# Two score buffers shared with the transposes, one PSUM bank for state products and y, and a new order of steps

## The chip, the cores and the metric

The kernel runs on one core of a Trainium2 chip. A core has five engines that work side by side, each through its own list of instructions in order: TensorE (PE in the profile; its weight loads are PEld), VectorE (DVE), ScalarE (ACT), GpSimd (POOL) and SyncE (SP), which here only issues DMAs. Matmul results go to PSUM, which has eight banks of 2 KB per partition; the other operands lie in SBUF. The metric is the time of the kernel on the device in microseconds, lower is better.

## The reference

An attention without softmax, with a decaying state, runs along the sequence, and a layer norm with a two-layer network follows. There are 4 batches, 8 heads, 768 positions and 48 values per head; the model width is 8 x 48 = 384.

```python
for t in range(S):
    kt, vt, rt = (k[:, :, t].copy(), v[:, :, t].copy(), r[:, :, t].copy())
    cur = np.einsum('bhd,bhe->bhde', u[None] * kt, vt)
    y[:, :, t] = np.einsum('bhd,bhde->bhe', rt, state + cur)
    state = w[None, :, :, None] * state + np.einsum('bhd,bhe->bhde', kt, vt)
...
xn = (x - mu) / np.sqrt(var + 1e-06) * g_ln
ch = np.maximum(xn @ w_ch1, 0.0) @ w_ch2
return (x + ch).astype(np.float32)
```

## The kernel before

The sequence of each batch is cut into 6 chunks of 128 positions: 24 chunks, numbered 0 to 23. Two neighbouring chunks make a pair, 12 pairs. Within a chunk the recurrence is computed as masked products of r and k (scores) times v; between chunks the state is handed on. The first two pairs (chunks 0 to 3) are worked on together with steps of their own, whose names end in 2. Then the chunk's rows pass through the network, in 18 groups of one or two chunks.

The steps that the text names, by chunk i, pair g or group:

- LK, LR, LV, LK2, LR2, LV2 load k, r and v; LW1 loads a third of the first weight matrix, SW scales one slice of it to bf16 (three slices to a third, so LW1,2 feeds SW,6 to SW,8), IW2 loads the second matrix by a DMA from GpSimd's queue. WF, UF and LG load w, u and the norm's gain. CV2 casts v.
- SK, SR, SK2, SR2 multiply k and r by powers of w. TRk and TRr transpose the results on TensorE into PSUM, TCk and TCr copy them to SBUF; from pair 5 on, TDk and TDr transpose by DMA instead. Q2 multiplies the two transposes.
- AT and AT2 compute the scores of one chunk (8 or 16 matmuls into two banks), AM and AM2 mask them into SBUF (VectorE). S computes the state product of a chunk, and for a pair's first chunk also the diagonal terms; CC2 copies those out, VB2 multiplies v by them, ZU and ZD make the next state.
- Y and Y2 compute y of a chunk, X adds VB2's part and sums the row, SQ the squares, XN centres the row, RS makes the norm's factor. LT transposes the row on TensorE and XT copies it out; from group 8 on, LTD does it by DMA.
- UP is one bank of the first matrix product (index 16 x group + part), RL its relu into SBUF, DN a third of the second product of a chunk (index 4 x chunk + part), OT scales and adds, STO stores. DU are filler matmuls on zeros that nothing waits for; WBM and COL spread w over the partitions at the start.

The order is written out by hand in the string PLAN (lines 18 to 66): `name,index,engine`, where the engine is v (VectorE), s (ScalarE), g (GpSimd) or - (TensorE, or a DMA on SyncE's queue). Lines 751 to 753 emit the steps in this order, so each engine gets its list in the order of PLAN, and semaphores make a step wait for its inputs and for the last readers of the buffer that it writes.

PSUM before: `hp` has two buffers of one bank (UP), `at` one buffer of two banks (AT, AT2), and one bank each go to `tr` (TRk, TRr, LT), `s` (COL, S), `y` (WBM, Y, Y2) and `o` (DU, DN). That makes eight.

Of the kernel before, what the change touches and what calls it, by code (L numbers as in the profile page):

```python
# [28 lines left out]
XT,3,v SW,4,s AT,6,- CC2,2,s SK,9,g RL,32,v UP,48,- SQ,0,s LV,8,- AM,6,v UP,50,- RL,48,s SW,3,g TRk,4,- SQ,2,s RL,50,v  # L29
UP,34,- IW2,1,g TCk,4,s LK,11,- SR2,4,v AT,7,- UP,1,- IW2,2,g RL,34,s VB2,2,v TRr,4,- RL,1,s DN,0,- ZU,4,v Q2,3,g LR2,5,-  # L30
TCr,4,s UP,33,- X,4,v AM,7,v XN,4,s Y,5,- UP,49,- RL,33,s CV2,3,v LT,4,- UP,17,- RL,49,s X,5,v XT,4,s S,6,- XN,5,g
RS,2,s Y,6,- AT,8,- ZU,6,v SQ,4,s UP,66,- RS,0,g AM,8,v CC2,3,s RL,17,s DN,1,- SQ,3,s LK,10,- S,7,- VB2,3,v LT,5,-
AT,9,- SQ,5,s DN,2,- X,6,v UP,64,- LR2,6,- OT,0,v XN,6,g Y,7,- RL,64,s Q2,4,v DN,4,- RL,66,s X,7,v RS,3,g LK,13,-
DN,5,- SQ,1,s XT,5,v DN,6,- SQ,6,s SR2,5,v UP,65,- LV,9,- RS,1,s LT,6,- XN,7,s OT,1,v UP,80,- SK,10,g RL,65,s ZU,7,v
DN,8,- LR2,7,- XT,6,s AM,9,v SK,11,g UP,82,- RS,4,g DN,9,- LK,12,- RL,80,v DN,10,- ZD,7,g LV,11,- UP,81,- CV2,4,s OT,2,v
SR2,6,g TRr,5,- TDk,5,- RL,82,v RS,5,s S,8,- TCr,5,s DN,12,- ZU,8,v DN,13,- RL,81,v SK,13,g LV,10,- CC2,4,s LT,7,- DN,14,-
SK,12,g XT,7,v TRr,6,- LV,12,- OT,3,v UP,114,- VB2,4,g TCr,6,v UP,112,- STO,0,- S,9,- RL,114,v Y,8,- ZD,8,g AT,10,- X,8,v
DN,16,- TDk,6,- Q2,5,g ZU,9,v XN,8,s DN,17,- AM,10,v CV2,5,s LV,13,- Y,9,- DN,18,- STO,2,- SQ,8,s X,9,v LK,15,- UP,96,-
ZD,9,g STO,1,- OT,4,v AT,11,- RL,96,s S,10,- Q2,6,v DN,20,- RL,112,s AM,11,v XN,9,g CC2,5,s DN,21,- VB2,5,g LTD,8,- UP,98,-
ZU,10,v DN,22,- RL,98,s SR2,7,v Y,10,- CV2,6,s UP,113,- STO,3,- ZD,10,g SQ,7,s UP,97,- OT,5,v LK,14,- LR2,8,- RL,113,v AT,12,-  # L40
RS,6,g RL,97,s DN,24,- LK,17,- X,10,v SQ,9,s RS,7,g S,12,- Y,11,- LV,14,- DN,25,- X,11,v UP,128,- XN,10,v XN,11,s LK,16,-
AM,12,v SK,14,g UP,129,- RL,128,s DN,26,- LTD,9,- SK,15,g RL,129,s UP,130,- OT,6,v UP,131,- SR2,8,v RL,130,s TRr,7,- RS,8,s CC2,6,v
RL,131,v DN,28,- VB2,6,g TDk,7,- ZU,12,v DN,29,- TCr,7,v DN,30,- AT,13,- SK,16,g OT,7,v UP,133,- LV,15,- UP,132,- LK,21,- RL,133,v
SK,17,g STO,4,- DN,32,- AM,13,v RL,132,s LV,16,- Y,12,- S,13,- STO,5,- DN,33,- X,12,v TDk,8,- AT,14,- Q2,7,v TRr,8,- UP,147,-
ZU,13,v TCr,8,s ZD,13,v DN,34,- RL,147,v XN,12,s Y,13,- UP,145,- OT,8,v CV2,7,s LR,19,- X,13,v UP,149,- RL,145,s XN,13,g S,14,-
SQ,12,s RL,149,v DN,36,- LTD,10,- SQ,11,s CC2,7,v AM,14,v UP,146,- VB2,7,g DN,37,- RL,146,s ZU,14,v AT,15,- SQ,10,s Y,14,- ZD,14,g
LV,17,- AM,15,v DN,38,- STO,6,- UP,144,- Q2,8,g LR,18,- X,14,v LK,20,- S,15,- AT,16,- OT,9,v RL,144,s LK,18,- Y,15,- RS,9,s
UP,148,- X,15,v SQ,13,s UP,164,- SK,21,g AM,16,v RL,148,s LR,20,- DN,40,- CV2,8,g ZU,15,v UP,161,- LK,19,- RL,164,v SR,19,g AT,17,-
RL,161,s S,16,- UP,160,- XN,14,s XN,15,v ZD,15,v DN,41,- RL,160,s LTD,11,- AM,17,v DN,42,- CC2,8,s UP,165,- ZU,16,v SK,18,g Y,16,-
OT,10,v UP,163,- STO,7,- RL,165,v SK,20,g LV,18,- DN,44,- RL,163,s STO,8,- VB2,8,v DN,45,- LV,19,- UP,162,- ZD,16,g X,16,v DN,46,-  # L50
RL,162,s SR,18,v UP,177,- RS,10,s OT,11,v XN,16,g TDr,9,- Y,17,- RL,177,s SK,19,g UP,180,- X,17,v SQ,15,s DN,48,- RL,180,v TDk,9,-
SQ,14,s DN,49,- CV2,9,g XN,17,s UP,178,- LR,21,- RS,11,g DN,50,- RL,178,s LTD,12,- UP,176,- SQ,16,s OT,12,v UP,179,- SR,20,v STO,9,-
RL,176,v DN,52,- TDk,10,- RL,179,s Q2,9,v DN,53,- SR,21,v DN,54,- AT,18,- S,18,- AM,18,v TDr,10,- UP,181,- UP,193,- RL,181,s ZU,18,v
AT,19,- OT,13,v RL,193,s Y,18,- UP,192,- STO,10,- AM,19,v CC2,9,s SQ,17,s LV,21,- DN,56,- LV,20,- S,19,- RL,192,v UP,194,- STO,11,-
VB2,9,v LV,23,- DN,57,- RL,194,s LK,23,- DN,58,- Q2,10,g X,18,v UP,195,- XN,18,s OT,14,v AT,20,- Y,19,- DN,60,- X,19,v CV2,10,g
DN,61,- AM,20,v XN,19,s DN,62,- SQ,18,s LTD,13,- ZU,19,v UP,197,- SQ,19,s OT,15,v ZD,19,g AT,21,- RL,195,s S,20,- DN,64,- LR,23,-
CC2,10,s RL,197,s ZU,20,v VB2,10,g STO,12,- UP,196,- AM,21,v LK,22,- S,21,- Y,20,- STO,13,- RL,196,s DN,65,- LR,22,- ZD,20,g RS,12,s
X,20,v LV,22,- DN,66,- SK,23,g UP,209,- OT,16,v Y,21,- XN,20,g ZU,21,v RL,209,s UP,213,- SR,23,v LTD,14,- UP,208,- SK,22,g RL,213,s
DN,68,- RS,13,s RL,208,v TDk,11,- UP,211,- X,21,v DN,69,- SR,22,v XN,21,s TDr,11,- RL,211,s DN,70,- SQ,21,s UP,210,- OT,17,v STO,14,-
UP,212,- RL,210,v LTD,15,- DN,72,- RL,212,v DN,73,- CV2,11,v UP,224,- STO,15,- UP,225,- RL,224,v STO,16,- DN,74,- ZD,21,v STO,17,- UP,226,-  # L60
OT,18,v AT,22,- Q2,11,v RL,226,s DN,76,- AM,22,v RL,225,s DN,77,- SQ,20,s S,22,- DN,78,- RS,14,g ZU,22,v AT,23,- CC2,11,s OT,19,v
Y,22,- VB2,11,g UP,240,- AM,23,v STO,19,- DN,80,- ZD,22,g X,22,v DN,81,- SQ,22,s DN,82,- XN,22,v RL,240,s LTD,16,- Y,23,- OT,20,v
UP,241,- RS,16,s X,23,v DN,84,- RL,241,s XN,23,v UP,242,- LTD,17,- RS,15,s SQ,23,s DN,85,- RL,242,v RS,17,s STO,18,- UP,258,- UP,256,-
RL,258,v DN,86,- RL,256,s UP,257,- OT,21,v UP,273,- STO,21,- RL,257,s STO,20,- DN,88,- RL,273,s DN,89,- UP,272,- DN,90,- RL,272,s UP,274,-
# [719 lines left out]
```

## Time and profile before

| | |
|---|---|
| median of three runs | 152.55 us (152.27 to 152.99) |
| the profiled execution | 152.22 us, of which the span from first to last instruction is 150.4 us |
| TensorE busy | 143.7 us, 96% of the span, 1960 matmuls |
| VectorE, ScalarE, GpSimd busy | 113.2, 83.1, 76.4 us |
| DMA | 26.92 MB, mean 179 GB/s, 16 DMA engines full in the first quarter of the span |
| TensorE clock granted | full speed throughout |

In the rows of the profile, a line such as `L545 PE MATMUL at<-trr,trk` names the source line, the engine, the operation and the tile written from the tiles read; then come the shapes, the count, the busy time in us with the mean of one in ns, and the idle time of the engine before them with what ended it. A timeline row begins with the start and the duration in us, counted from the first instruction; it merges neighbours of one kind, and the idle time before it stands in brackets. Matmuls overlap, so what a step costs TensorE is the distance from its start to the start of the next step.

### The profile page before, as it was taken

To read this page: it belongs to the slowest core of one execution; us is meant where nothing else is said; L and a number is where in the kernel's file an instruction comes from. 1 tells how busy PE (TensorE), PEld (TensorE's weight loads), DVE (VectorE), ACT (ScalarE), POOL (GpSimd) and SP (SyncE) were. 2 spreads that over 40 slices of the span, in tenths; PEclk is the share of its full clock that TensorE was granted. 3 is DMA by queue.
4 is the path that set the end of the run, shared out by engine and by line. 5 is a ranking of instruction groups with operands and counts; after the bars stand their busy time and mean duration, and the time that the engine had idled before them with its cause. 6 is when DMAs were issued, how large, how long until landed. Compare 5 with 4: busy or idle time off the path is not lost.

```text
span 150.4 us, 4721 instructions
## 1 busy us (share of the span) xinstructions
PE 143.7 (96%) x1960; PEld 112.5 (75%) x1963; DVE 113.2 (75%) x203; ACT 83.1 (55%) x185; POOL 76.4 (51%) x94
## 2 busy tenths in 40 slices
...
GB/s 106 309 314 324 290 242 261 215 196 257 233 211 160 65 166 167 160 195 179 124 213 175 138 148 196 198 188 187 187 188 67 241 160 185 140 52 52 118 91 56
DMA packets 84041, 26.92 MB, mean 179 GB/s; under 512 B 79282, under 2 KB 82484, under 8 KB 84020
## 3 DMA queue, kind: packets, MB, share of 16 engines
...
q10 hardware_dynamic: 402, 0.00, 0.2%
...
HBM read 18.88 MB, written 4.72 MB: 157 GB/s over the span
## 4 chain that ended last, share of the span: by engine, by line
PE 94%; DVE 4%; issue 1%
PE hp L647 31%; PE o L675 30%; PE o L271 6%; PE at L545 4%; PE tr L392 4%; PE s L482 3%; PE y L584 3%; PE y L505 2%; PE y L576 2%; PE s L461 2%; DVE xn L607 2%; PE at L435 1%; PE tr L632 1%; DVE A L554 1%; PE o L273 1%; PE o L690 1%
## 5 line engine op out<-in xcount | busy, mean ns | idle before, releaser
L647 PE MATMUL hp<-xT,w_sb 128*128 128x128 bf16 (+1 forms) x648 | 57.1, 237 | 0.0
L647 PEld LDWEIGHTS <-w_sb 128*128 128x128 bf16 x648 | 49.4, 114 | 4.0
L675 PE MATMUL o<-w_sb,hT 128*128 128x384 bf16 x276 | 52.4, 326 | 0.0
L663 ACT ACTIVATE hT<-hp 128x512 bf16<-128x512 f32 x49 | 28.9, 596 | 36.7 <-PE hp L647 36.4
L675 PEld LDWEIGHTS <-hT 128*128 128x128 bf16 x276 | 25.3, 98 | 12.5
L554 DVE TENSOR_TENSOR A<-at,mask 128x1024 bf16<-128x1024 f32 x20 | 24.4, 1218 | 1.3 <-PE at L545 1.3
L731 DVE SCALAR_TENSOR_TENSOR ot<-o,rs,x 128x384 f32<-128x384 f32 x23 | 14.2, 616 | 11.7 <-PE o L675 10.5
L202 POOL TENSOR_TENSOR sk<-kf,Fk 128x384 bf16<-128x384 f32 x18 | 19.1, 1075 | 5.7 <-ACT g_neg L296 4.8
L665 DVE TENSOR_SCALAR hT<-hp 128x512 bf16<-128x512 f32 x23 | 15.8, 688 | 4.8 <-PE hp L647 4.6
L591 DVE SCALAR_TENSOR_TENSOR x<-y,Vb 128x384 f32<-128x384 f32 x24 | 13.3, 553 | 5.2 <-PE y L584 3.0
L598 ACT ACTIVATE sqj<-x,sm 128x384 bf16<-128x384 f32 x24 | 14.7, 612 | 2.4 <-DVE x L591 2.2
L493 POOL TENSOR_TENSOR Vb<-vf,cc 128x768 f32<-128x768 f32 x8 | 11.8, 1480 | 8.0 <-ACT cc L197 4.1
L202 POOL TENSOR_TENSOR q<-trk,trr 128x1024 bf16<-128x1024 bf16 x5 | 10.7, 2138 | 6.7 <-DMA trr<-sr 6.7
L607 POOL TENSOR_SCALAR xn<-x,sm 128x384 bf16<-128x384 f32 x8 | 4.9, 614 | 17.9 <-DVE x L591 15.1
L271 PE MATMUL o<-warm 128*128 128x512 bf16 x31 | 10.2, 458 | 1.5 <-DVE warm L221 1.5
L605 ACT ACTIVATE xn<-x,sm 128x384 bf16<-128x384 f32 x11 | 6.8, 615 | 8.4 <-DVE x L591 8.4
L202 POOL TENSOR_TENSOR Z<-ZS,WLZ 128x384 bf16<-128x384 f32 x9 | 9.8, 1084 | 2.8 <-DVE ZS L566 2.8
L197 ACT COPY trr<-tr 128x512 bf16<-128x512 bf16 (+1 forms) x11 | 7.7, 766 | 5.9 <-PE tr L392 5.9
L202 DVE TENSOR_TENSOR sr<-rf,Fr 128x384 bf16<-128x384 f32 (+1 forms) x12 | 9.1, 764 | 2.2 <-ACT Fr L290 2.2
L202 POOL TENSOR_TENSOR sr<-rf,Fr 128x768 bf16<-128x768 f32 (+1 forms) x4 | 6.7, 1682 | 2.9 <-DMA rf<-in_r_dram 2.9
L566 DVE TENSOR_TENSOR ZS<-s,Z 128x384 f32<-128x384 f32 x12 | 6.6, 552 | 1.8 <-ACT cc L197 1.0
L545 PE MATMUL at<-trr,trk 48*128 48x128 bf16 x160 | 7.9, 219 | 0.0
...
## 6 DMA issues: line engine op xcount, KB each, us to landing
...
```

Source lines behind the costliest of these rows:

```text
L202: engines[e].tensor_tensor(out=out, in0=in0, in1=in1, op=ALU.mult)
L271: nc.tensor.matmul(out=warm_ps[0][:], lhsT=warm[:, :P], rhs=warm[:], start=True, stop=True)
L493: engines[e].tensor_tensor(out=Vb2(g).rearrange("p (x h d) -> p x h d", x=2, h=H), in0=vals, in1=cc2(g)[:].unsqueeze(3).to_broadcast([P, 2 ...
L545: nc.tensor.matmul(out=t[:, par, q, :], lhsT=trk(g)[p0 : p0 + D, a, q, :], rhs=trr(g)[p0 : p0 + D, a, q, :], start=True, stop=True,)
L554: nc.vector.tensor_tensor(out=AA(i)[:].rearrange("p e q t -> p (e q) t"), in0=psum["at", i][:].rearrange("p e q t -> p (e q) t"), in1=mask ...
L591: nc.vector.scalar_tensor_tensor(out=xx(i)[:], in0=psum["y", i][:, :C], scalar=1.0, in1=Vb(i), op0=ALU.mult, op1=ALU.add, accum_out=sm[i][:],)
L598: nc.scalar.activation(out=sqj[:], in_=xx(i)[:], func=ACT.Square, bias=sm[i][:], scale=-float(C), accum_out=sq[g][:, j : j + 1])
L647: nc.tensor.matmul(out=t[:, a * gw : (a + 1) * gw], lhsT=w1_sb[n][kc][:, fb::FB], rhs=xT(g)[:, :size, kc, :], start=(kc == 0), stop=(kc == ...
L663: nc.scalar.activation(out=o, in_=s, func=ACT.Relu)
L665: nc.vector.tensor_relu(out=o, in_=s)
L675: nc.tensor.matmul(out=psum["o", i][:, :C], lhsT=hT(g)[:, fk, j * P : (j + 1) * P], rhs=w2_sb[d][:, a, :], start=(fk == 0), stop=(fk == FK ...
L731: nc.vector.scalar_tensor_tensor(out=ot(i)[:], in0=psum["o", i][:, :C], scalar=rs[g][:, j : j + 1], in1=xx(i)[:], op0=ALU.mult, op1=ALU.add,)
```

## The change

PSUM is divided anew. `at` gets two buffers of two banks in a pool of its own, `ps_a`, and the transposes (TRk, TRr, LT) take their tiles from the same two buffers, of which they use half. S and Y share the one bank `y`. Y2, WBM and COL take their tiles from the two `hp` banks of the up-projection. `o` stays as it is. The sum is again eight banks.

PLAN has the same 749 steps in a new order. 113 of them change their engine or queue, among them: ten SK from GpSimd to VectorE and two the other way; three SW from ScalarE to VectorE and two to GpSimd (SW,0, SW,6 and SW,8 are on VectorE now, SW,1 to SW,3 on GpSimd); four ZD to VectorE and one from it; XN in 15 cases on GpSimd now, 6 on ScalarE and 3 on VectorE (before: 8, 11 and 5); three TCr from VectorE to ScalarE; 13 RL from VectorE to ScalarE and 11 the other way. The fillers DU keep their number and sizes. 16 of the 20 AT stand in pairs, one right behind the other on TensorE.

```diff
 PLAN = """
...
-LK2,0,- MP,4,g MM2,0,g LV2,0,- LN,0,s UWR,0,v DU,2176,- MP,3,v MO,0,v CV2,1,v LK2,1,- WBM,0,- COL,0,- LR2,1,- FR2,1,s FR2,0,s
-DU,2640,- SRH,1,v FK2,1,s SRH,0,v LK,5,- FK2,0,s UW,0,v SKH,1,v TRr,0,- UGC,0,s MP,0,v SKH,0,g DU,3120,- FR,0,s LR2,2,- TCr,0,v
-FK,0,s WL,0,s TRk,0,- LW1,0,- SK2,1,v DU,3616,- LV,5,- TCk,0,s SR2,1,v CV2,0,s LR2,3,- TRk,1,- AT2,0,- SK,4,v TCk,1,s Q2,0,v
-SK,5,v LW1,2,- S,0,- AM2,0,v SR2,2,g DU,576,- CC2,0,s TRr,1,- ZU,0,v TCr,1,s AT2,1,- LK,6,- DU,784,- AM2,1,v VB2,0,g S,1,-
-DU,576,- SW,0,s LK,7,- TRr,2,- ZU,1,v Y2,0,- TCr,2,s Q2,1,v AT2,2,- X,0,v DU,704,- SW,2,s LV,4,- TRk,2,- AM2,2,v XN,0,g
-Y2,1,- TCk,2,s SR2,3,g DU,576,- X,1,v AT2,3,- SW,1,s LT,0,- DU,464,- AM2,3,v S,2,- XT,0,s LW1,1,- XN,1,s UP,0,- LK,8,-
-ZU,2,v SW,7,s LT,1,- AT,4,- CC2,1,s SK,6,v LK,9,- XT,1,s Y2,2,- AM,4,v VB2,1,g SW,6,s S,3,- SW,8,s TRr,3,- ZU,3,v
-AT,5,- SK,7,g X,2,v TCr,3,s UP,16,- RL,0,v LR2,4,- Y2,3,- XN,2,g RL,16,s Q2,2,g TRk,3,- CV2,2,s X,3,v UP,18,- TCk,3,s
-AM,5,v UP,2,- LV,6,- RL,18,s LT,2,- XN,3,v IW2,0,g Y,4,- SW,5,s XT,2,v S,4,- RL,2,s LT,3,- SK,8,g LV,7,- UP,32,-
...
+SKH,0,v FR2,1,s SKH,1,g MP,5,v MP,0,v FR2,0,s DU,3120,- LV2,1,- UW,0,v WL,0,s SRH,1,v SRH,0,v TRk,0,- LR2,3,- SR2,1,v TRr,0,-
+TCk,0,s DU,3616,- LW1,0,- SR2,2,v LK,5,- TCr,0,s SK2,1,v TRr,1,- LV,5,- AT2,0,- TCr,1,s Q2,0,v DU,576,- AM2,0,v FK,0,s S,0,-
+FR,0,s AT2,1,- LK,7,- CC2,0,v ZU,0,v DU,784,- UGC,0,s VB2,0,g CV2,1,s TRk,1,- AM2,1,v S,1,- TCk,1,s DU,576,- SR2,3,v TRr,2,-
+LV,4,- Y2,0,- SK,4,v TCr,2,s SW,2,g ZU,1,v AT2,3,- LK,6,- Q2,1,v Y2,1,- SW,1,g X,0,v LW1,1,- TRr,3,- AM2,3,v LV,6,-
+SK,5,g S,2,- TCr,3,s LW1,2,- DU,704,- XN,0,g ZU,2,v LV,7,- X,1,v LT,0,- DU,576,- SW,0,v XT,0,s DU,464,- TRk,2,- CC2,1,s
+SQ,0,s AT2,2,- SK,6,g UP,0,- TCk,2,s AM2,2,v VB2,1,g S,3,- XN,1,s LR2,4,- RL,0,v AT,4,- CV2,2,s Y2,2,- ZU,3,v SK,7,g
+RS,0,s AM,4,v Y2,3,- SW,5,s SW,3,g SW,4,s Q2,2,v TRk,3,- LK,9,- X,2,v LT,1,- S,4,- TCk,3,s XT,1,v XN,2,g UP,1,-
+X,3,v CC2,2,v ZU,4,v UP,16,- XN,3,g RL,1,s IW2,0,g AT,5,- LK,8,- Y,4,- SW,8,v SW,7,s VB2,2,g SW,6,v LT,2,- RL,16,s
+AM,5,v UP,18,- LR2,5,- XT,2,s UP,2,- RL,18,s X,4,v LT,3,- Q2,3,v UP,34,- RL,2,s LV,9,- XN,4,g XT,3,v Y,5,- RL,34,s
+AT,6,- SR2,4,g X,5,v AT,7,- CV2,3,s UP,48,- AM,6,v UP,33,- RL,48,s LV,8,- SK,9,v S,6,- IW2,1,g RL,33,s UP,17,- ZU,6,v
...
+RL,208,s Y,20,- RL,211,s DN,64,- X,20,v SQ,19,s UP,212,- XN,20,g S,21,- SK,23,g DN,65,- ZU,21,v UP,209,- SK,22,v CV2,11,g RL,212,v
+Y,21,- TDk,11,- RL,209,s DN,66,- UP,210,- OT,16,v STO,13,- UP,213,- X,21,v RL,210,s DN,68,- XN,21,s RL,213,s DN,69,- LTD,15,- Q2,11,v
+RS,13,s DN,70,- ZD,21,v STO,14,- S,22,- OT,17,v AT,23,- LTD,14,- AT,22,- ZU,22,v DN,72,- AM,22,v DN,73,- STO,15,- DN,74,- CC2,11,v
...
@@ -101,6 +101,7 @@
     ps_h = ctx.enter_context(tc.tile_pool(name="ps_h", bufs=2, space=bass.MemoryType.PSUM))
+    ps_a = ctx.enter_context(tc.tile_pool(name="ps_a", bufs=2, space=bass.MemoryType.PSUM))
     ps = ctx.enter_context(tc.tile_pool(name="ps", bufs=1, space=bass.MemoryType.PSUM))
...
     def WBM(i, e):
-        t = psum["wb"] = ps.tile([P, 512], FP32, name="y")
+        t = psum["wb"] = ps_h.tile([P, 512], FP32, name="hp")
...
     def COL(i, e):
-        t = psum["col"] = ps.tile([P, 2, HP], FP32, name="s")
+        t = psum["col"] = ps_h.tile([P, 512], FP32, name="hp")[:, : 2 * HP].rearrange("p (a q) -> p a q", a=2)
...
     def turn(key, t):
-        psum[key] = ps.tile([P, 2 * HP, P], BF16, name="tr")
+        psum[key] = ps_a.tile([P, 4 * HP, P], BF16, name="at")[:, : 2 * HP, :]
...
     def AT2(i, e):
-        t = psum["at", i] = ps.tile([P, 2, HP, P], FP32, name="at")
+        t = psum["at", i] = ps_a.tile([P, 2, HP, P], FP32, name="at")
...
     def S_(i, e):
-        t = psum["s", i] = ps.tile([P, 512], FP32, name="s")
+        t = psum["s", i] = ps.tile([P, 512], FP32, name="y")
...
     def Y2(i, e):
-        t = psum["y", i] = ps.tile([P, 512], FP32, name="y")
+        t = psum["y", i] = ps_h.tile([P, 512], FP32, name="hp")
...
     def AT(i, e):
-        t = psum["at", i] = ps.tile([P, 2, HP, P], FP32, name="at")
+        t = psum["at", i] = ps_a.tile([P, 2, HP, P], FP32, name="at")
...
     def LT(i, e):
-        t = psum["lt", i] = ps.tile([P, 2 * HP, P], BF16, name="tr")
+        t = psum["lt", i] = ps_a.tile([P, 4 * HP, P], BF16, name="at")
```

More of the change, by code (lines that the diff above doesn't have):

```diff
@@ L28 @@
-AM,5,v UP,2,- LV,6,- RL,18,s LT,2,- XN,3,v IW2,0,g Y,4,- SW,5,s XT,2,v S,4,- RL,2,s LT,3,- SK,8,g LV,7,- UP,32,-
[L29 to L62, printed above, removed]
@@ L63 @@
[L63 to L64 removed]
+WF,0,s MP,1,g LR2,0,- MW,0,v MM2,0,g MZ,0,v LK2,0,- UF,0,s DU,3800,- MP,4,v MP,3,v LV2,0,- MO,0,v TL,0,s MM,0,g LR2,1,-
+MP,2,g MI2,0,g MI,0,g LK2,1,- LN,0,s DU,2176,- WBM,0,- LG,0,- UWR,0,g LR2,2,- DU,2640,- FK2,0,s LK,4,- CV2,0,v FK2,1,s COL,0,-
@@ new lines @@
+SK,8,v TRr,4,- CC2,3,s LK,11,- RL,17,s VB2,3,g UP,50,- AM,7,v TCr,4,s UP,49,- LK,10,- RL,50,v LT,4,- IW2,2,g Y,6,- TRk,4,-
+XT,4,s SR2,5,v SQ,5,s DN,0,- XN,5,g RL,49,v LR2,6,- UP,32,- SQ,4,s X,6,v TRr,5,- TCk,4,s S,7,- UP,65,- ZU,7,v SQ,1,s
+Q2,4,g RL,32,v LT,5,- DN,1,- TCr,5,s UP,64,- RL,65,v Y,7,- RL,64,s AT,8,- CV2,4,g X,7,v LR2,7,- DN,2,- XN,6,s XT,5,v
+SQ,2,s ZD,7,g UP,66,- OT,0,v SQ,6,s LK,13,- S,8,- AM,8,v XN,7,g UP,80,- SQ,3,s SK,10,g LT,7,- RL,66,s DN,4,- LV,10,-
+RS,4,s SK,11,v DN,5,- XT,7,s SR2,6,g ZU,8,v RS,3,s DN,6,- CC2,4,v RL,80,v LV,11,- RS,1,s Y,8,- OT,1,v UP,82,- VB2,4,v
```

27 lines of the change are left out of this document (26 added, 1 removed).

## The prediction

> **What bounds the kernel now.** I read the page first, then the busy time by stage, then who TensorE waited for, then the timeline of the few places where it did wait.
>
> ```profile
> span 150.4 us, 4721 instructions
> PE 143.7 (96%) x1960; PEld 112.5 (75%) x1963; DVE 113.2 (75%) x203; ACT 83.1 (55%) x185; POOL 76.4 (51%) x94
> 0.00:9.00 9.00, 7.49 (x53) 3.41 (x55) 3.42 (x15) 3.64 (x6) 3.42 (x21) 1.00 0.89 227
> 9.00:22.70 13.70, 13.19 (x256) 9.38 (x257) 12.24 (x20) 10.80 (x20) 7.12 (x5) 1.00 1.07 287
> 22.70:33.00 10.30, 8.73 (x207) 7.65 (x205) 8.41 (x13) 8.97 (x18) 8.62 (x9) 1.00 1.00 226
> 33.00:147.40 114.40, 114.30 (x1454) 92.07 (x1452) 88.80 (x157) 59.67 (x144) 57.23 (x61) 1.00 0.74 161
> PE tr L632 <- DVE xT L199: 1.6, 1, 1.6
> ```
>
> The rows with a colon are stages: length, busy time of PE, PEld, DVE, ACT, POOL, granted clock, DMA share, GB/s. TensorE bounds the kernel, at the full clock throughout. From 33.0 to 147.4 us it is busy 114.3 of 114.4, so no buffer can take a wait away there. Its one long wait is 1.6 us, at a transpose. What remains to win is the opening up to 33 us (partly filler matmuls, DMA busy throughout), that wait, and matmul steps that cost more than they need. What can be lost is larger: every wait that the new buffers bring in after 33 us counts in full, because TensorE has no idle time there to hide it. The wait in the timeline:
>
> ```profile
> 28.77 1.22 DVE L554 TENSOR_TENSOR A<-at,mask 128x1024 bf16<-128x1024 f32 x1
> 29.46 0.79 POOL L341 DMA_DIRECT2D w_sb<-in_moe_w_ch_dram  x1
> 29.90 2.56 DVE L607 TENSOR_SCALAR xn<-x,sm 128x384 bf16<-128x384 f32 x1
> 30.27 1.96 POOL L202 TENSOR_TENSOR sk<-kf,Fk 128x384 bf16<-128x384 f32 x2
> 32.23 0.79 POOL L338 TENSOR_SCALAR w_sb<-w_f,g_neg 128x512 bf16<-128x512 f32 x1
> 32.38 0.34 DVE L199 COPY xT<-tr 128x384 bf16<-128x384 bf16 x1
> 32.78 0.33 PE L632 MATMUL tr<-ident,xn 128*128 128x128 bf16 x3 [1.57 <-DVE xT L199]
> ```
>
> LT,3 needs the one transpose bank; XT,2 must empty it; XT,2 is queued on VectorE behind XN,3, which took 2.56 us. XN,3 began while GpSimd was issuing IW2,0 and ended 0.23 us after GpSimd's next two operations. So a VectorE instruction between SBUF tiles can be held by GpSimd, and here through three of its instructions in a row.
>
> **Prices of the steps.** Starts on TensorE, one after another, give what each step costs there:
>
> ```profile
> 24.04 0.91 PE y L505 x40
> 35.57 0.45 PE tr L392 x8
> 60.94 0.83 PE L647 MATMUL hp<-xT,w_sb 128*128 128x128 bf16 x12
> 61.71 0.40 PE L545 MATMUL at<-trr,trk 48*128 48x128 bf16 x8
> 62.04 0.35 PE L461 MATMUL s<-uwI,q 128*128 128x2 bf16 x8
> 62.42 1.46 PE L675 MATMUL o<-w_sb,hT 128*128 128x384 bf16 x8
> 63.72 0.83 PE L647 MATMUL hp<-xT,w_sb 128*128 128x128 bf16 x12
> 64.39 0.81 PE L675 MATMUL o<-w_sb,hT 128*128 128x384 bf16 x4
> 65.04 0.33 PE L576 MATMUL y<-Z,trr 128*128 128x96 bf16 x4
> L545 PE MATMUL at<-trr,trk 48*128 48x128 bf16 x160 | 7.9, 219 | 0.0
> ```
>
> UP 0.67 (63.72 to 64.39), DN 0.65, AT 0.33, S 0.38, Y2 0.91, TR 0.45, Y about 0.37. But the UP that AT follows took 0.77 (60.94 to 61.71): entering AT costs 0.10 more. AT comes 160/8 = 20 times, always alone.
>
> **Score buffers, pairs.** With two `at` buffers the new order puts 16 of the 20 AT next to each other (6 and 7, 10 and 11, to 22 and 23): eight entries fewer, -0.8 us, all on TensorE. That two AT in a row share one entry isn't shown by this trace; if leaving the step costs as much as entering it, or each needs its own, the gain lies between 0 and -0.8. I take -0.8, because AT always takes 0.33 and the step behind it never shows an extra. A pair needs both buffers free: the shortest way from an AT to the next user of its buffer is 2.8 us of TensorE work (TRr,6 behind AT,9), against AM's 1.22; no price.
>
> **Transposes in `at`, XN,3 and XT,2.** LT,3 no longer shares one bank with XT,2; XN,3 goes to GpSimd and XT,2 to ScalarE. This wait, 1.6 us, goes. What is late next decides the opening, so I walked the new order from 13 us by hand, each engine taking its own list in order. A reader of a matmul's result starts 0.2 after the last matmul of the step begins (a matmul lasts 219 ns, row above), any other follower 0.06 after its input (32.38 + 0.34 to 32.78). The rows of the longest lists:
>
> ```profile
> 13.83 1.23 DVE L526 TENSOR_TENSOR A<-at,mask 128x1024 bf16<-128x1024 f32 x1
> 14.97 0.55 DVE L202 TENSOR_TENSOR Z<-s,WLZ 128x384 bf16<-128x384 f32 x1
> L202 DVE TENSOR_TENSOR q<-trk,trr 128x1024 bf16<-128x1024 bf16 x7 | 4.8, 683 | 0.0
> L665 DVE TENSOR_SCALAR hT<-hp 128x512 bf16<-128x512 f32 x23 | 15.8, 688 | 4.8 <-PE hp L647 4.6
> L591 DVE SCALAR_TENSOR_TENSOR x<-y,Vb 128x384 f32<-128x384 f32 x24 | 13.3, 553 | 5.2 <-PE y L584 3.0
> L202 DVE TENSOR_TENSOR sk<-kf,Fk 128x384 bf16<-128x384 f32 x4 | 2.2, 553 | 0.0
> L493 POOL TENSOR_TENSOR Vb<-vf,cc 128x768 f32<-128x768 f32 x8 | 11.8, 1480 | 8.0 <-ACT cc L197 4.1
> L607 POOL TENSOR_SCALAR xn<-x,sm 128x384 bf16<-128x384 f32 x8 | 4.9, 614 | 17.9 <-DVE x L591 15.1
> 16.80 0.61 PE L392 MATMUL tr<-ident,sr 128*128 128x128 bf16 x8
> 22.68 0.52 PE L647 MATMUL hp<-xT,w_sb 128*128 128x128 bf16 x6
> ```
>
> A VectorE instruction frees its engine about 0.08 before its end (13.83 to 14.97 for 1.23). The fillers DU are the same in number and size. VectorE (us): AM2,0 13.8, ZU,0 15.0, AM2,1 15.5, SR2,3 16.6, SK,4 17.5, ZU,1 17.9, Q2,1 18.4, X,0 19.0, AM2,3 19.5, ZU,2 20.9, X,1 21.4, SW,0 21.9, AM2,2 22.8, RL,0 23.9, ZU,3 24.5, AM,4 25.0, Q2,2 26.1, X,2 26.7, X,3 27.5, ZU,4 28.1, SW,8 28.5, SW,6 29.0, AM,5 29.5, X,4 30.6, Q2,3 31.1. TensorE: TRr,2 16.7 (before: 16.80), UP,0 22.6 (before: 22.68), Y2,2 24.4, S,4 26.9, UP,1 27.6, AT,5 29.0, Y,4 29.4, UP,18 30.0, LT,3 31.3, S,6 34.7 to 35.1. By then it has done all that stood before LT,3 at 32.78, and four UP, LT,3, Y,5, AT,6, AT,7 and S,6: 2.68 + 0.16 + 0.37 + 0.66 + 0.38 + one entry 0.10 = 4.35 us. The old order is there at 32.78 + 4.35 = 37.1. The opening gains 2.0, if nothing holds VectorE, which in this stretch is nearly full.
>
> The loads are reordered too. The first third of W1 has 192 KB more ahead of it (LR2,3 is now before it, LK,5 behind it), 0.7 us at 287 GB/s, and isn't needed before SW,2 at 17. The last third is now the 18th large load instead of the 13th: 6.7 MB with its own 768 KB. The stages moved 9.0 x 227 + 13.7 x 287 KB = 6.0 MB by 22.7, and the rest takes 3.3 us at 226 GB/s, so it lands near 26, ahead of SW,8. WF goes from SyncE's queue to ScalarE's and LG the other way; WBM stands behind the fillers in both orders. No price.
>
> **W1 scaling on VectorE.** SW,0, SW,8 and SW,6 come to VectorE: 0.42 to 0.69 each, between the quickest form of this kind (row below) and RL; I take 0.5, nearest to the former. They are `tensor_scalar` from SBUF to SBUF, as XN,3 was. Behind X,3 GpSimd runs XN,3 (28.2 to 28.8), IW2,0 (0.79) and VB2,2 (1.48) without a gap until 31.0, and SW,8 comes at 28.5. If it is held as XN,3 was, it ends near 31.2 and SW,6 at 31.7; UP,18 needs both and starts at 31.8 instead of 30.0. Queued behind them are AM,5, for which LT,3's buffer waits, and X,4. Price 0 to 1.8; I take 1.8, since IW2,0 is the same instruction that started the old wait.
>
> ```profile
> 136.85 0.42 DVE L607 TENSOR_SCALAR xn<-x,sm 128x384 bf16<-128x384 f32 x1
> 63.05 1.48 POOL L493 TENSOR_TENSOR Vb<-vf,cc 128x768 f32<-128x768 f32 x1 [1.23 <-ACT cc L197]
> 63.88 1.46 DVE L202 TENSOR_TENSOR sr<-rf,Fr 128x768 bf16<-128x768 f32 x1
> 64.48 1.73 POOL L202 TENSOR_TENSOR Z<-ZS,WLZ 128x384 bf16<-128x384 f32 x1
> trk<-sk SPq DMA_TRANSPOSE x7, 3.6
> ```
>
> The Trainium skill ("SBUF — State Buffer", section "Who interferes with whom") says that the two engines share a port pair as an exclusive lock, held for one whole instruction by whichever issues first. The row at 63.88 agrees: 1.46 us, ending 0.8 after Vb, between two GpSimd instructions. The row at 29.90 doesn't: it was held through three.
>
> **SK and ZD to VectorE, XN to GpSimd.** Ten SK and four ZD go to VectorE (14 x 0.55), one ZD, two SK, two RL, three TCr and others leave it; its sum stays near 113. They read SBUF only, so each may be held like the row at 63.88. Before, such holds cost TensorE nothing after 33 us. Price 0 to 1.3; the upper end is a whole VB2 (1.48) less the 0.2 that VectorE idles before ZU,2. I take 0.6, about what the row at 63.88 waited for Vb to end (64.53): SR2,3, SK,4 and Q2,1 stand in the full opening beside SW,2 and SW,1 on GpSimd.
>
> **One bank for S and Y.** S, then CC2 and ZU, then Y, then X, each waits for the last. Between the closest (S,21 behind Y,20; Y,21 behind S,21; Y,12 behind Y,11) lie two DN or UP, 1.3 us; a reader needs 0.55 and some 0.3 around it. Taken at 0; the cover is 0.4 wide, and a VectorE that is late by an AM (1.22) would break it by 0.8. Y2 in the `hp` banks: UP,1 and UP,16 wait for X,2 and X,3 at 27.5 and 28.3; under 0.1.
>
> **TDk,11 and Q2,11.** They now stand 3.3 us of TensorE work apart, before 7.5. The transpose lands in 3.6 (row above) and its issue waits for SK,22. Q2,11 holds VectorE for the landing, with ZD,21 and OT,17 behind it, and S,22 waits: 0 to 1.5, I take 0.5 (3.6 less 3.3, and the issue).
>
> **The sum** against the profiled 152.22 (span 150.4): -0.8 - 2.0 + 1.8 + 0.6 + 0.5 = +0.1. That execution is 0.33 below the median 152.55, so on the median 152.65, say 152.7. About 0.5% (0.76 us) is what a measurement here can tell from no change.
>
> **Rivals.** First, GpSimd lets SW,8 in when XN,3 ends, as the row at 63.88 was let in: the 1.8 shrinks to 0.2, -1.5 in sum, 151.1; without the 0.6 it is 150.5. Against it stands the row at 29.90. That is also how the rule of the Trainium skill, named above, would have it.
>
> Second, slower: SW,0 loses to VB2,1. On VectorE SW,0 comes at 21.9; VB2,1 can start at 22.1, after CC2,1. If VectorE is 0.2 late and GpSimd first, SW,0 waits for its 1.48, and if SK,7 and SW,3 follow without a gap, for 3.3. UP,0, the first up-projection, waits as long, with nothing under it: +1.6 to +3.4, 154.3 to 156.1. It decides from a lateness of 0.2.
>
> Third, slower as well, the shared bank binds: VectorE late by an AM at four of the 1.3 us places, 4 x 0.8 = +3.2, 155.9; at two, 154.3. For it: 33 hand-overs on one bank. Against: 88.8 of 114.4 busy, and covers of 1.0 to 1.3 (two UP or DN) already held for `hp` and `o`.
>
> **Chances.** Forecast 0.34, first rival 0.28, second 0.22, third 0.16. Of the forecast's own, 0.28 lies within 0.5%, 0.02 below and 0.04 above. Faster 0.30, same 0.28, slower 0.42. The range runs from the first rival without the 0.6 and with half of TDk,11's 0.5, 150.2, to the second with 2.5 us, 155.2; the forecast's own is 151.6 to 153.6.
>
> **What would show it.** AT in pairs with one entry each; no wait at LT,3; TensorE unbroken after about 37 us. Right if SW,8 on VectorE lasts over 1.5 us and UP,18 waits for it; the first rival if it lasts under 0.8. UP,0 later than 23.5 is the second rival. Waits of S or Y for X or ZU past 40 us are the third. Wrong altogether if the opening is late before 20 us.

## The result: 0.9% faster, and the profile after

The changed kernel takes 151.31 us (median of 13 runs) where the kernel before takes 152.55 (13 runs beside them): a ratio of 0.9914, interval 0.9886 to 0.9942. The forecast was no change. Medians here and below are of all runs; ratios and intervals leave out executions that took over 1.5% longer than the fastest of their kernel. The profiled execution of the changed kernel took 151.62 us, its span is 149.9; before it was 152.22 and 150.4. Line numbers are one higher than before from line 101 on.

First the head of the page of the changed kernel and its long stage (length, then busy time of PE, PEld, DVE, ACT, POOL, granted clock, DMA share, GB/s):

```profile
span 149.9 us, 4734 instructions
PE 142.5 (95%) x1963; PEld 112.7 (75%) x1963; DVE 111.2 (74%) x204; ACT 83.6 (56%) x185; POOL 75.1 (50%) x93
33.00:147.40 114.40, 112.47 (x1450) 92.19 (x1447) 85.60 (x154) 62.38 (x149) 55.82 (x57) 1.00 0.75 160
```

TensorE still bounds the kernel, but from 33 us on it is busy 112.5 of 114.4, where it had been 114.3. So there are waits in that stretch which the kernel before did not have, and the span is shorter all the same: the matmul steps must have become cheaper. Whom TensorE waited for in the changed kernel (total, times, longest):

```profile
PE hp L648 <- DVE w_sb L337: 1.5, 1, 1.5
PE o L676 <- DMA w_sb<-in_moe_w_ch_dram: 1.2, 1, 1.2
PE o L272 <- DVE warm L222: 1.2, 1, 1.2
PE at L393 <- POOL sk L203: 0.2, 1, 0.2
```

The third is the start of the kernel and stood before too (1.5 us). The first is the wait that was forecast: an up-projection waits for a slice of W1. The second was not forecast: DN,2 waits for the last third of W2. The transpose's wait of 1.6 us is gone.

**The forecast wait.** The timeline of the changed kernel, VectorE, GpSimd and TensorE, 28.6 to 33 us:

```profile
28.64 0.59 POOL L608 TENSOR_SCALAR xn<-x,sm 128x384 bf16<-128x384 f32 x1 [0.26 <-DVE cc L200]
28.90 2.85 DVE L337 TENSOR_SCALAR w_sb<-w_f,g_neg 128x512 bf16<-128x512 f32 x2
29.17 0.79 POOL L342 DMA_DIRECT2D w_sb<-in_moe_w_ch_dram  x1
29.98 1.48 POOL L494 TENSOR_TENSOR Vb<-vf,cc 128x768 f32<-128x768 f32 x1
31.68 1.21 DVE L555 TENSOR_TENSOR A<-at,mask 128x1024 bf16<-128x1024 f32 x1
31.81 1.53 PE L648 MATMUL hp<-xT,w_sb 128*128 128x128 bf16 x24 [1.48 <-DVE w_sb L337]
28.90 0.60 DVE L337 TENSOR_SCALAR w_sb<-w_f,g_neg 128x512 bf16<-128x512 f32 x1
```

The second row holds SW,8 and SW,6; the last row is SW,8 alone, from the same view over a shorter window. SW,8 comes while GpSimd runs XN,3, is let in when XN,3 ends (29.23) and is done at 29.50. SW,6 takes the remaining 2.3 us: it comes while GpSimd issues IW2,0, and it ends 0.3 after VB2,2 (31.46). UP,18 starts at 31.81.

**The unforeseen wait.** GpSimd issues W2's last third (IW2,2) at 39.37, behind VB2,3. TensorE is ready for DN,2 first. GpSimd and TensorE in the timeline of the changed kernel, then the landing times of the three W2 loads from the view of line 342, then the issue of the last two thirds in the kernel before:

```profile
36.17 0.61 POOL L342 DMA_DIRECT2D w_sb<-in_moe_w_ch_dram  x1
39.37 0.59 POOL L342 DMA_DIRECT2D w_sb<-in_moe_w_ch_dram  x1
44.79 0.40 PE L546 MATMUL at<-trr,trk 48*128 48x128 bf16 x8
46.44 0.49 PE L676 MATMUL o<-w_sb,hT 128*128 128x384 bf16 x2 [1.25 <-DMA w_sb<-in_moe_w_ch_dram]
```

```profile
DMA to landing us min/median/max: 6.0/6.7/7.0
```

```profile
32.98 1.14 POOL L341 DMA_DIRECT2D w_sb<-in_moe_w_ch_dram  x2
```

AT,8 takes 1.65 us to the next step instead of 0.33, since the third load, issued at 39.37, is in 7.0 later, at about 46.4. The kernel before had issued it by 34.1.

**What a pair costs.** AT,10 and AT,11 in the timeline of the changed kernel, and the group row of all its AT:

```profile
58.15 0.81 PE L676 MATMUL o<-w_sb,hT 128*128 128x384 bf16 x4
58.89 0.62 PE L546 MATMUL at<-trr,trk 48*128 48x128 bf16 x16
59.44 0.75 PE L648 MATMUL hp<-xT,w_sb 128*128 128x128 bf16 x10
```

```profile
L546 PE MATMUL at<-trr,trk 48*128 48x128 bf16 x160 | 6.7, 218 | 0.0
```

DN in front of the pair takes 0.74 (58.15 to 58.89), its 0.65 and one entry. But the pair takes 0.55 (58.89 to 59.44), not 2 x 0.33 = 0.66. So the 0.33 of a lone AT held some 0.10 for going back to the matmuls of the next step, and a pair saves that as well as an entry: 0.20 us, not 0.10. The group's busy time fell from 7.9 to 6.7 with the number of matmuls unchanged.

### The profile page after: what moved, and what is told of

It is laid out like the page before. It is cut to its first block, busy times and chain, and to the rows that moved or that the text cites. A ratio compares the mean times of both kernels' runs of the same rounds, so it can differ in the third digit from the quotient of the medians.

```text
span 149.9 us, 4734 instructions
## 1 busy us (share of the span) xinstructions
PE 142.5 (95%) x1963; PEld 112.7 (75%) x1963; DVE 111.2 (74%) x204; ACT 83.6 (56%) x185; POOL 75.1 (50%) x93
## 4 chain that ended last, share of the span: by engine, by line
PE 84%; DVE 6%; DMA 5%; issue 3%; POOL 1%
PE o L676 29%; PE hp L648 28%; PE o L272 7%; DMA w_sb<-in_moe_w_ch_dram 5%; PE at L546 3%; PE at L393 3%; PE y L483 2%; PE y L585 2%; DVE w_sb L337 2%; PE y L577 2%; PE hp L506 1%; PE y L462 1%; PE at L436 1%; DVE A L527 1%; DVE q L203 1%
## 5 line engine op out<-in xcount | busy, mean ns | idle before, releaser
L494 POOL TENSOR_TENSOR Vb<-vf,cc 128x768 f32<-128x768 f32 x10 | 14.8, 1477 | 26.5 <-DVE cc L200 15.9
L608 POOL TENSOR_SCALAR xn<-x,sm 128x384 bf16<-128x384 f32 x15 | 10.0, 669 | 12.4 <-DVE x L592 10.7
L592 DVE SCALAR_TENSOR_TENSOR x<-y,Vb 128x384 f32<-128x384 f32 x20 | 11.1, 553 | 4.5 <-PE y L585 4.2
L198 ACT COPY trr<-at 128x512 bf16<-128x512 bf16 (+1 forms) x16 | 11.4, 782 | 4.4 <-PE at L393 4.4
L203 POOL TENSOR_TENSOR sk<-kf,Fk 128x384 bf16<-128x384 f32 x10 | 10.1, 1006 | 4.8 <-ACT Fk L294 2.6
L203 POOL TENSOR_TENSOR Z<-ZS,WLZ 128x384 bf16<-128x384 f32 x6 | 6.4, 1064 | 10.9 <-DVE ZS L567 9.9
L203 POOL TENSOR_TENSOR q<-trk,trr 128x1024 bf16<-128x1024 bf16 x4 | 8.5, 2132 | 4.7 <-DMA trr<-sr 2.7
L203 DVE TENSOR_TENSOR sk<-kf,Fk 128x384 bf16<-128x384 f32 (+1 forms) x13 | 8.2, 637 | 0.3 <-ACT Fk L294 0.3
L567 DVE TENSOR_TENSOR ZS<-y,Z 128x384 f32<-128x384 f32 x12 | 6.6, 553 | 2.3 <-PE y L483 2.0
L272 PEld LDWEIGHTS <-warm 128*128 128x128 bf16 x34 | 3.5, 112 | 5.7 <-issue 2.8
```

What stands on the lines that cost most here:

```text
L198: nc.scalar.copy(out=out, in_=in_)
L203: engines[e].tensor_tensor(out=out, in0=in0, in1=in1, op=ALU.mult)
L272: nc.tensor.matmul(out=warm_ps[0][:], lhsT=warm[:, :P], rhs=warm[:], start=True, stop=True)
L494: engines[e].tensor_tensor(out=Vb2(g).rearrange("p (x h d) -> p x h d", x=2, h=H), in0=vals, in1=cc2(g)[:].unsqueeze(3).to_broadcast([P, 2 ...
L592: nc.vector.scalar_tensor_tensor(out=xx(i)[:], in0=psum["y", i][:, :C], scalar=1.0, in1=Vb(i), op0=ALU.mult, op1=ALU.add, accum_out=sm[i][:],)
```

## The experiments

The theory after the traces, still to be tested here: the gain comes from the pairs, at 0.20 each, 1.6 us in all. What else the new order wins in the opening it gives back at two places of GpSimd's queue: SW,6's hold (1.5) and IW2,2 (1.2). The rivals: that the pairs bring only the forecast 0.8 and the rest is the opening; and for the hold, that VectorE is kept out by any unbroken run of GpSimd instructions ("chain"), or that GpSimd's DMA issue has a part in it ("issue"). All edits but the sixth's are to the changed kernel, and each only reorders PLAN. Ratios are to the kernel before, run beside each; experiments are compared with each other and with the changed kernel by these ratios (1% is 1.5 us), since the kernel before had a median of 153.1 beside the first four, 153.5 beside the next three and 152.9 beside the last.

**First: split the pairs.** The two AT of each of the eight pairs are parted by the TensorE step next to them; nothing else moves. One of the eight:

```diff
-AT,10,- AT,11,- SQ,8,s SR2,7,g OT,3,v UP,96,-
+AT,10,- UP,96,- SQ,8,s SR2,7,g OT,3,v AT,11,-
```

> The changed kernel with the second score step of each of the eight pairs moved behind the next TensorE step; nothing else differs. If a pair saves one entry of 0.10 us (my theory), eight entries come back: +0.8 us against the changed kernel, ratio to the old kernel 0.997 instead of 0.991, and eight more steps ahead of a score step that last 0.10 longer. Rival: the pairs save nothing and the gain came from the opening; then the time stays at 0.991.

Measured: 154.33 us, ratio 1.0084 (1.0053 to 1.0115): slower than the kernel before, and 1.7% (2.6 us) above the kernel with pairs. The same stretch in its timeline:

```profile
59.60 0.40 PE L546 MATMUL at<-trr,trk 48*128 48x128 bf16 x8
59.93 0.86 PE L648 MATMUL hp<-xT,w_sb 128*128 128x128 bf16 x12
60.72 0.40 PE L546 MATMUL at<-trr,trk 48*128 48x128 bf16 x8
61.05 0.35 PE L462 MATMUL y<-uwI,q 128*128 128x2 bf16 x8
```

Two AT and an UP take 1.45 (59.60 to 61.05: 0.33 + 0.79 + 0.33) where the pair and its UP take 1.25 in the changed kernel (58.89 to 60.14): 0.20 lost. Step by step the eight splits cost 0.20 to 0.28, 1.8 us together. One wait is new behind the first split, at 96.4:

```profile
PE hp L648 <- DVE hT L666: 0.3, 1, 0.3
```

DN,2, on the other hand, waits 0.99 instead of 1.25. From the start of UP,0 to the last matmul the profiled execution is 2.4 us longer than the changed kernel's: 1.8 by the splits, 0.3 less 0.25 by these two waits, and 0.6 in small delays that aren't explained here. What follows: without the pairs the change is no gain at all, so the pairs carry it. That a pair is worth twice the price that I gave it rests on the steps, not on the whole 2.6.

**Second: a gap for the W1 slices.** CC2,2 goes behind SW,6 on VectorE, so that VB2,2, which needs it, cannot start on GpSimd before both slices are done; IW2,0 goes behind VB2,2.

```diff
-X,3,v CC2,2,v ZU,4,v UP,16,- XN,3,g RL,1,s IW2,0,g AT,5,- LK,8,- Y,4,- SW,8,v SW,7,s VB2,2,g SW,6,v LT,2,-
+X,3,v ZU,4,v UP,16,- XN,3,g RL,1,s AT,5,- LK,8,- Y,4,- SW,8,v SW,7,s SW,6,v CC2,2,v VB2,2,g IW2,0,g LT,2,-
```

> The changed kernel with GpSimd kept idle while VectorE scales W1: CC2,2 goes behind SW,6 on VectorE, so VB2,2 can't start before, and IW2,0 goes behind VB2,2. SW,8 and SW,6 stay on VectorE. If GpSimd's operations held SW,6 (2.33 us), it now takes about 0.5, the wait of UP,18 (1.5 us) falls under 0.3, and the kernel gains 1.5 us: ratio 0.981. Rival: the weights land late or VectorE's own list is late; then UP,18 still waits over 1 us and the ratio stays near 0.991.

Measured: 150.59 us, ratio 0.9839 (0.9807 to 0.987), 1.1 us below the changed kernel's. Both slices together, on VectorE:

```profile
29.50 1.07 DVE L337 TENSOR_SCALAR w_sb<-w_f,g_neg 128x512 bf16<-128x512 f32 x2
```

1.07 instead of 2.85, and UP,18 waits for them no longer. The step from AT,5 to UP,18 fell by 1.0 (from 2.52 to 1.51), not by the whole 1.5: in this profile AT,5 itself breaks off for 0.4 after five of its matmuls. Far ahead of the edit's place this execution has another wait:

```profile
PE at L633 <- POOL xn L608: 1.4, 1, 1.4
```

That is LT,0 at 22.2. W1's first third landed at 18.77 instead of 16.24 in the changed kernel's profile, and on GpSimd XN,0, which LT,0 needs, now stands behind SW,2 and SW,1, which need that third. The opening of the new order is the same in eight of the profiled executions: in five of them GpSimd waits 0.7 to 3.0 us for this load, and in three of these LT,0 waits (1.4, 0.4 and 0.5, in the second, fourth and fifth experiments). All of it lies ahead of the edits.

**Third: W2 early.** IW2,1 and IW2,2 follow VB2,2 at once.

```diff
-SW,8,v SW,7,s VB2,2,g SW,6,v
+SW,8,v SW,7,s VB2,2,g IW2,1,g IW2,2,g SW,6,v
```

> The changed kernel with the second and third load of W2 issued right behind VB2,2 on GpSimd, near 31.5 us instead of 36.2 and 39.4. If only the issue was late, DN,2 no longer waits (1.25 us before) and the kernel gains 1.2 us: ratio 0.983. Rival: the load is paid by the others, since the DMA engines are full until 40 us; then r, k or v of chunks 8 to 13 come late, a wait of about the same size stands elsewhere, and the ratio stays near 0.991.

Measured: 151.12 us, ratio 0.9859 (0.9814 to 0.9904). All its waits of TensorE:

```profile
PE hp L648 <- DVE w_sb L337: 1.4, 1, 1.4
PE o L272 <- DVE warm L222: 1.2, 1, 1.2
```

DN,2's wait is gone and the slices' has stayed. From S,6 to DN,2 TensorE takes 8.6 us instead of 10.0. By the ratios it is 0.8 us, and the two intervals overlap.

**Fourth: both.** The second edit with all three IW2 behind VB2,2.

> Both edits together: GpSimd idle while VectorE scales W1, then VB2,2 and all three loads of W2 in a row. If the two waits are independent, the gains add to 2.7 us: ratio 0.973, no wait of TensorE over 0.3 us behind 20 us. Rival: the first gain only makes DN,2 come earlier than the weights, and the sum is under 2 us.

Measured: 149.99 us, ratio 0.9779 (0.9742 to 0.9817), faster than both kernels, the intervals well apart. Its waits of TensorE:

```profile
PE o L272 <- DVE warm L222: 1.2, 1, 1.2
PE at L633 <- POOL xn L608: 0.4, 1, 0.4
PE y L462 <- DVE q L203: 0.3, 1, 0.3
PE at L546 <- issue: 0.2, 1, 0.2
```

Neither of the two long waits is left. The two places of GpSimd's queue thus cost the changed kernel 1.35%, 2.1 us, against 1.1 and 0.8 for each alone. That is less than the 2.7 expected and a little more than the rival's 2. The wait of 0.4 is LT,0 again, behind W1's first third.

**Fifth: no issue between XN,3 and VB2,2.** Why does SW,6 wait through VB2,2 when SW,8 was let in? Only IW2,0 moves, behind VB2,2.

```diff
-XN,3,g RL,1,s IW2,0,g AT,5,- LK,8,- Y,4,- SW,8,v SW,7,s VB2,2,g SW,6,v
+XN,3,g RL,1,s AT,5,- LK,8,- Y,4,- SW,8,v SW,7,s VB2,2,g IW2,0,g SW,6,v
```

> The changed kernel with IW2,0 behind VB2,2 on GpSimd, so that VB2,2 follows XN,3 at once and no DMA is issued between them. Theory 'issue': it is GpSimd's issue of IW2,0 during which VectorE's request is lost, and the operation behind the issue goes first; without it a waiting VectorE instruction is let in at the end of the GpSimd instruction that runs. Then SW,8 (asked at 28.9, in XN,3) is let in near 29.2 and takes about 0.6, SW,6 is asked at 29.4 in VB2,2 and ends about 0.5 after it, near 31.1: 1.7 us; UP,18 starts near 31.2 instead of 31.8. Theory 'chain': VectorE stays out as long as GpSimd goes on without a gap, DMA issue or not. Then SW,8 itself is held, 1.8 to 2.1 us, to about 31.0, and SW,6 takes 0.5 behind it. The time differs little between them, 150.7 to 151.3; what tells them apart is which of the two slices is the long one.

Measured: 150.69 us, ratio 0.987 (0.9748 to 0.9993). The interval holds the changed kernel's 0.9914, so the time tells nothing; the timeline does:

```profile
28.76 0.60 DVE L337 TENSOR_SCALAR w_sb<-w_f,g_neg 128x512 bf16<-128x512 f32 x1
29.05 1.64 POOL L494 TENSOR_TENSOR Vb<-vf,cc 128x768 f32<-128x768 f32 x1
29.29 1.69 DVE L337 TENSOR_SCALAR w_sb<-w_f,g_neg 128x512 bf16<-128x512 f32 x1
31.03 1.53 PE L648 MATMUL hp<-xT,w_sb 128*128 128x128 bf16 x24 [0.40 <-DVE w_sb L337]
```

SW,8 (28.76) passes between XN,3 and VB2,2, which follow each other on GpSimd without a gap, and VB2,2 is 0.16 longer for it; SW,6, which comes during VB2,2, waits until it ends (30.69) and is done at 30.98. "Chain" has fallen: VectorE is let in at the end of the GpSimd operation that runs when it asks.

**Sixth: the same in the kernel before.** There XN,3 on VectorE took 2.56 us. IW2,0 goes behind SK,9.

```diff
-XN,3,v IW2,0,g Y,4,- ... SK,8,g ... SK,9,g RL,32,v
+XN,3,v Y,4,- ... SK,8,g ... SK,9,g IW2,0,g RL,32,v
```

> The kernel before with IW2,0 behind SK,9 on GpSimd and nothing else changed. XN,3 on VectorE is asked near 29.9 as before, now while GpSimd runs SK,8 (then SK,9, then IW2,0). Theory 'issue' (the DMA issue is what lost XN,3 its turn; else a VectorE instruction is let in at the end of the one that runs): XN,3 takes 0.7 to 1.2 instead of 2.56, LT,3's wait of 1.6 falls under 0.4, and the time is 1.2 to 1.6 below the kernel before, ratio 0.990 to 0.993. Theory 'chain' (out as long as GpSimd goes on without a gap): XN,3 lasts until SK,9 ends, 1.6 to 1.9 us, LT,3 waits 0.7 to 1.0, and the time is 0.6 to 0.9 below, ratio 0.994 to 0.996.

Measured: 152.55 us, ratio 0.9967 (0.9916 to 1.0018): no difference that can be told. Its timeline:

```profile
30.40 2.09 POOL L202 TENSOR_TENSOR sk<-kf,Fk 128x384 bf16<-128x384 f32 x2
30.83 0.79 DVE L607 TENSOR_SCALAR xn<-x,sm 128x384 bf16<-128x384 f32 x1
35.03 2.17 POOL L202 TENSOR_TENSOR q<-trk,trr 128x1024 bf16<-128x1024 bf16 x1
35.41 2.62 DVE L202 TENSOR_TENSOR sr<-rf,Fr 128x768 bf16<-128x768 f32 x1
38.08 0.62 PE L392 MATMUL tr<-ident,sr 128*128 128x128 bf16 x8 [1.08 <-DVE sr L202]
```

XN,3 takes 0.79 instead of 2.56, again let in between two GpSimd operations, and LT,3 waits no more; "issue" was right about which instruction gets in. The gain that it forecast doesn't show, though the interval still reaches into it (0.990 to 0.993). VectorE, now early, meets the next GpSimd operation: SR2,4 comes 0.4 into a Q2 of 2.17 us, is held until that ends (37.20), takes 2.62 instead of 0.95, and TRr,4 waits 1.08. In the kernel before SR2,4 came at 36.21, as Q2 ended. The hold had moved, not gone.

**Seventh: three issues in a row.** IW2,1 and IW2,2 directly behind IW2,0, ahead of VB2,2.

> The changed kernel with IW2,1 and IW2,2 right behind IW2,0 on GpSimd, ahead of VB2,2: three DMA issues in a row (0.6 to 0.8 each) lie between XN,3 and VB2,2, and VB2,2 starts near 31.2 instead of 30.0. If an issue alone does not hold VectorE (theories 'one instruction' and 'chain of tensor operations'): SW,8 about 0.6, SW,6 about 0.5 and done by 30.1, UP,18 near 30.2, its wait of 1.5 gone; and since W2 comes early, DN,2's 1.2 goes too: 149.8 to 150.4, ratio 0.980 to 0.984, the fourth experiment's gain without moving CC2,2. If an issue holds it, or loses it its turn until the next tensor operation has run (theory 'issue'): SW,6 ends after 31.3, perhaps only after VB2,2 at 32.7; then only DN,2's part is gained, or with VB2,2 later by 1.2 nothing: 150.6 to 152.

Measured: 151.01 us, ratio 0.9855 (0.9724 to 0.9985). The timeline of VectorE and GpSimd, and three of TensorE's waits:

```profile
29.02 0.99 DVE L337 TENSOR_SCALAR w_sb<-w_f,g_neg 128x512 bf16<-128x512 f32 x2
29.29 1.92 POOL L342 DMA_DIRECT2D w_sb<-in_moe_w_ch_dram  x3
31.22 1.50 POOL L494 TENSOR_TENSOR Vb<-vf,cc 128x768 f32<-128x768 f32 x1
```

```profile
PE y L577 <- DVE x L592: 0.7, 1, 0.7
PE y L483 <- DVE x L592: 0.5, 1, 0.5
PE y L577 <- DVE cc L200: 0.4, 1, 0.4
```

SW,8 waits for the end of XN,3 (0.60 in all) and SW,6, asked for inside the first issue (at 29.55), takes 0.47, so an issue by itself does not hold it. The ratio is some 0.3% above what was expected, though the interval is too wide to hold that against it; the trace shows where it would lie: VB2,2 is 1.2 later, X,4 waits for it, and Y,5 waits for X,4 on the shared bank. S,7 at 42 us waits there for X,6, and Y,8 at 50 us for CC2,4, which came late behind an SK that took 1.93 on VectorE. These are waits as the prediction's third rival had them, at three places, 1.6 us in all.

**Eighth: all of W2 behind VB2,2, CC2,2 left where it was.**

```diff
-SW,8,v SW,7,s VB2,2,g SW,6,v
+SW,8,v SW,7,s VB2,2,g IW2,0,g IW2,1,g IW2,2,g SW,6,v
```

> The changed kernel with all three issues of W2 (IW2,0, IW2,1, IW2,2) right behind VB2,2 on GpSimd; CC2,2 stays where the change put it. If a waiting VectorE instruction is let in at the end of the GpSimd operation that runs, unless a DMA issue stands between: SW,8 0.6 and SW,6 1.7 us (through VB2,2) as in the fifth experiment, LT,2 to UP,18 0.5 too long instead of 1.6; and W2's last third is issued near 32 instead of 39, so DN,2 waits for nothing. Against the changed kernel that is -1.1 and -1.3: 149.0 to 149.9, ratio 0.976 to 0.981, at least as good as the fourth experiment and without its late CC2,2. If the three issues in a row hold XN,4 or SR2,4 behind them on GpSimd, XN,4 ends after 33.5 and LT,4 or Y,6 shows a new wait: 150.0 to 150.8.

Measured: 151.19 us, six runs from 148.83 to 156.34, against 152.86; too scattered for an interval. In its waits of TensorE UP,18 stands thus:

```profile
PE hp L648 <- DVE w_sb L337: 0.8, 1, 0.8
```

The two slices take 2.21 as in the fifth, and DN,2, LT,4 and Y,6 are not among the waits; from UP,0 to DN,2 it takes 21.7 us, the changed kernel 23.8, the fourth experiment 21.4. So W2's part went as expected and the slices' only in part: LT,2 to UP,18 takes 1.17, 1.0 too long where 0.5 was expected. A wait of 0.8 at a Y2 (19.7 us), for which the profile names no releaser, lies ahead of the edit's place. The time is no evidence for or against it.

The profiled executions can be compared without their first 23 us, from the start of UP,0 to the start of the last matmul, one execution each: 124.4 us in the kernel before and 123.8 in the changed kernel; 126.3, 122.1, 122.1 and 121.4 in the first to the fourth experiment; 122.8, 122.8 and 121.8 in the fifth, the seventh and the eighth. By this too parting the pairs loses (2.4), curing either place of GpSimd's queue gains, and the fourth remains the best that is shown (2.4 under the changed kernel).

## Why the prediction was wrong

The forecast was 152.7, a net of +0.1 in the profiled execution; it was -0.6 there and -1.2 at the medians. Two steps of the prediction failed: the price of a pair was put at half of what it is, and the two loads of W2 that were moved were given no price. The median stands near the first rival's 151.1, but not by its mechanism: the wait of UP,18 that this rival takes away was there. By the steps of the sum:

**Pairs, forecast -0.8, measured -1.6** (8 x 0.20; the eight splits give 1.8). The mechanism was right, and this is the term that was mis-sized. The prediction named leaving cost as a reason for less ("if leaving the step costs as much as entering it ... the gain lies between 0 and -0.8"). That is backwards: a leaving cost is saved by a pair too. The argument that "AT always takes 0.33 and the step behind it never shows an extra" could not exclude it, because a leaving cost that every lone AT pays is part of its 0.33; nor is "never" quite so, since in the kernel before an UP behind an AT takes 0.70 instead of 0.67 (36.95 to 37.65). The rows of the prediction held the answer: at 61.71 eight matmuls of AT show 0.40, and one lasts 0.219, so the eighth starts 0.18 after the first, 0.026 from one to the next; but the step behind starts at 62.04, 0.15 after the eighth.

**The opening, forecast -2.0 and +1.8, measured about -0.3 together.** The walk held well. S,6 of the changed kernel:

```profile
36.41 0.34 PE L462 MATMUL y<-uwI,q 128*128 128x2 bf16 x8
36.78 0.61 PE L648 MATMUL hp<-xT,w_sb 128*128 128x128 bf16 x8
```

It is over at 36.78; forecast was 35.1 and the 1.8, 36.9, against 37.1 for the old order. UP,18 came at 31.81, to the tenth where it was put. That is in part luck: the slice that is held is SW,6 and not SW,8. SW,8 took 0.60, which by the prediction's own sign is the first rival: it was let in when XN,3 ended, and SW,6 then met IW2,0 and VB2,2. VB2,2 ended 0.5 later than the walk had it (31.46 instead of 31.0), and one slice instead of two had to follow it; the two errors cancel. The first rival's mechanism was right for one slice, and its gain still did not come.

**The other holds, forecast +0.6, measured about nothing on the path.** Two show (Q2,2 and TRk,3's wait of 0.2 to 0.4, behind SK,7 on GpSimd), and S,6 is not late by them.

**TDk,11 and Q2,11, forecast +0.5, measured 0.** VectorE did wait for the transposed tile:

```profile
124.06 0.69 DVE L203 TENSOR_TENSOR q<-trk,trr 128x1024 bf16<-128x1024 bf16 x1 [1.03 <-DMA trk<-sk]
```

It was done at 124.75, and S,22 begins at 125.00 with no wait among TensorE's.

**IW2, forecast nothing, measured +1.3.** The two later thirds of W2 were moved past SR2,4 and VB2,3 on GpSimd's queue, and the prediction gave that no sentence. It is the missing term; the third experiment, which moves these two issues, takes the wait away. "TensorE unbroken after about 37 us" failed by it.

**W1's first third, forecast nothing.** "Isn't needed before SW,2 at 17" was too narrow a cover: in the eight profiled executions that share this opening it landed between 16.2 and 18.8. In the changed kernel's own profile it came in time.

Behind S,6 the errors cancel: forecast -0.7 (seven of the pairs) and +0.5, -0.2; measured -1.4 and +1.3, -0.1. What made the difference in the profiled executions is therefore the 0.6 for holds that did not come, and the pair in the opening. The other 0.6 of the medians is in which executions were profiled: before's lay 0.33 under its median, after's 0.31 over. How far the first 13 us shift is seen from TRk,1, which begins at 12.70 in the kernel before and at 13.46 in the sixth experiment, which has the same order up to there: 0.76 us apart, before any edit of it acts. One span against another is good to no better than that. For the opening above it matters little, since UP,0 begins at 22.68 before and at 22.65 after.

**Rivals.** The second did not happen: UP,0 came at 22.65. The third shows at no place in the changed kernel, and at three places, for 0.7, 0.5 and 0.4, in the seventh experiment, which made VB2,2 late: the cover that I took at 0.4 wide is real and thin.

**Open.** In the kernel before XN,3, asked for during IW2,0, missed not only the operation behind the issue but the gap behind that one as well (SK,8 to SK,9). In the changed kernel SW,6 missed one. What an issue does to the order of turns is shown only as far as this: a `tensor_scalar` of VectorE, asked for during an issue with a GpSimd operation on SBUF right behind it, was passed over; with another issue behind it, or with no issue, it was not. It doesn't hold for every VectorE instruction. In the changed kernel SR2,5, a `tensor_tensor`, comes during IW2,2's issue (39.37 to 39.96) with XN,5 right behind:

```profile
39.66 1.22 DVE L203 TENSOR_TENSOR sr<-rf,Fr 128x768 bf16<-128x768 f32 x1
40.01 1.32 POOL L608 TENSOR_SCALAR xn<-x,sm 128x384 bf16<-128x384 f32 x1
```

SR2,5 was done at 40.88, 0.27 longer than its usual 0.95, and it was XN,5 that had to wait (1.32 instead of 0.59). The first, second and fifth experiments show the same. Whether the form of the VectorE instruction decides it is not tested. The break of 0.2 to 0.4 within AT,5 in the second, fourth and fifth experiments has no releaser in the profile, and CC2,2's place does not explain it, since in the fifth it is the old one.
